# The first W1 piece loaded ahead of the second x half, and five units' first slab done in column halves

## The chip, the cores and the metric

The kernel runs on one core of one Trainium2 chip. The metric is the device time of one execution in microseconds, the median of several runs. Engines: PE (matmul), DVE and ACT (elementwise, both can read PSUM), POOL (elementwise), SP (issues the DMAs). PE writes to PSUM, which has 8 banks of 512 fp32 columns; the next matmul into a bank has to wait until its content has been copied out.

## What is computed

The input x has 2048 rows (tokens) of D = 512. Two branches are mixed by a gate for each token:

```python
g = sigmoid((x * gate_w).sum(-1, keepdims=True))
# a: linear attention, 32 heads of 16
q, k, v = split(x @ wqkv)                       # per head
phi = lambda t: concat(softmax(t @ w_phi), softmax(-(t @ w_phi)))
kv, z = phi(k).T @ v, phi(k).sum(tokens)        # per head
a = concat_heads((phi(q) @ kv) / (phi(q) @ z + 1e-6)) @ wo
# b: dense branch, Dff = 1376
b = relu(x @ w1) @ w2
out = g * a + (1 - g) * b
```

All inputs and the output are bf16.

## The kernel before

The program is planned engine by engine. `p.op(engine, fn, after, ev)` appends one instruction to an engine's list, with the events it waits for and the event it sets; `p.dma` does the same for a DMA issue. Each engine runs its list strictly in the order of the calls, so an instruction that waits holds up everything behind it on its engine. `p.early(engine)` moves what was listed so far on that engine ahead of the engine's wait in the start barrier. `free[bank]` names the event after which a PSUM bank may be written again.

The tokens are handled in four chunks of 512 columns of XT, which is x transposed (four blocks `t` or `dt` of 128 rows of D). Chunks 1 to 3 are transposed by DMA. Chunk 0, which the kernel starts with, is transposed on PE: x is loaded row-wise into XS in two halves `h` (256 tokens each, `loadx0`, L162), PE multiplies blocks of 128 x 128 with an identity matrix into PSUM (`xtr`, L239), and DVE (L255) or ACT (L258) copy them into XT as bf16. There are 16 such transposes, 8 for each half of x. Until the first half of x is there, PE runs matmuls on a constant tile (`warm`, L232).

Then comes the dense branch of chunk 0 for its first eight units `u` of 128 columns of W1: `slab(t)` (L528) runs, for one block `t` of D, one 512-column matmul for each unit, into the bank `UB[u]`, where

```python
UB = (3, 4, 5, 0, 6, 7, 2, 1)
```

Four slabs accumulate in the eight banks; in slab 0 a unit first has to wait until its bank's transposes have been copied out. W1 comes in pieces (`loadw1`, L166): the columns of units 0 to 3 of block 0 (event `w10a`), those of units 4 to 7 of block 0 (`w10`), then blocks 1 to 3 one by one. After slab 3 `relu` copies each bank to HT, and the rest follows: further units (`hunit`, L282), v (`vtile`, L411), the products of weights (`pre`, L316), attention tiles (`atile`, L336), and at the end the output products (`finB`, L490, and `finA`, L499).

The order on PE in the opening is: five warm matmuls, the gate column (L225), one more warm matmul, six transposes of the first half of x, two of the second, two of the first, four of the second, slab 0 for units 0 to 3, the last two transposes of the second half, slab 0 for units 4 to 7, slabs 1 to 3. The transposes lie in banks 6, 7, 2, 1 and again 2, and DVE and ACT make three copies each: DVE of 256 columns each, ACT of 256, 512 and 512.

Of the kernel before, what the change touches and what calls it, by code (L numbers as in the profile page):

```python
# [5 lines left out]
ACT = mybir.ActivationFunctionType  # L6
# [62 lines left out]
def bass_gated_mix__linear_kernel_hedgehog__dense_activation_relu__prompt_kernel(  # L69
# [17 lines left out]
    P = 128  # L87
    NT = S // P
    NDT = D // P
# [15 lines left out]
    with ExitStack() as es:  # L105
        E = es.enter_context
        XT = E(nc.sbuf_tensor("XT", [P, NDT, S], BF16))
# [6 lines left out]
        W1 = E(nc.sbuf_tensor("W1", [P, NDT, DFF + 8], BF16))  # L114
# [11 lines left out]
        IDN = E(nc.sbuf_tensor("IDN", [P, P], BF16))  # L126
# [14 lines left out]
        PS = E(nc.psum_tensor("PS", [P, 8, 512], FP32))  # L141

        XS = OT[:, 0, :].rearrange("p (j d) -> p j d", j=4)
# [7 lines left out]
        p = _Plan(["sp", "pool", "act", "dve", "pe"])  # L151
        free = {b: [] for b in range(8)}
# [8 lines left out]
        def loadx0(h):  # L161
            p.dma("sp", lambda e: e.dma_start(out=XS[:, 2 * h:2 * h + 2, :], in_=xq[:, 2 * h:2 * h + 2, :]),  # L162
                  f"x0{h}", ev=f"x0{h}")

        def loadw1(t, c0=0, c1=DFF, tag=""):
            p.dma("sp", lambda e: e.dma_start(  # L166
                out=W1[:, t, c0:c1], in_=B_w1[t * P:(t + 1) * P, c0:c1]), f"w1{t}{tag}", ev=f"w1{t}{tag}")
# [1 line left out]
        p.dma("act", lambda e: e.dma_start(out=GR[0:NDT, :], in_=gate_w.rearrange("(j p) -> j p", p=P)),  # L169
              "gr", after=["grz"], ev="gr")  # L170
        p.early("act")
        for h in range(2):
            loadx0(h)
        p.early("sp")
        loadw1(0, 0, 4 * P, "a")
        loadw1(0, 4 * P, 8 * P)
        for t in range(1, NDT):
            loadw1(t, 0, 8 * P)
        p.dma("sp", lambda e: e.dma_start(
            out=W1[:, :, 8 * P:DFF], in_=B_w1[:, 8 * P:DFF].rearrange("(j p) n -> p j n", p=P)), "w1r", ev="w1r")  # L180
        p.dma("sp", lambda e: e.dma_start(
            out=WPS[:, :, :], in_=A_w_phi.rearrange("(g hl) r c -> (hl r) g c", g=NDT)), "wps", ev="wps")
        p.dma("sp", lambda e: e.dma_start(
            out=WV[:, :, :], in_=A_wqkv[:, 2 * D:3 * D].rearrange("(j p) n -> p j n", p=P)), "wv", ev="wv")
        for i in range(2):
            p.dma("sp", lambda e, i=i: e.dma_start_transpose(
                out=WQKT[:, 4 * i:4 * i + 4, :], in_=A_wqkv[:, i * D:(i + 1) * D]), f"wqk{i}", ev=f"wqk{i}")
        for c in range(1, NCH):
            p.dma("sp", lambda e, c=c: e.dma_start_transpose(
                out=XT[:, :, c * 512:(c + 1) * 512], in_=x2[c * 512:(c + 1) * 512, :]), f"x{c}", ev=f"x{c}")  # L190
# [9 lines left out]
            after=["wps"], ev="wd")  # L200
        for gt in range(NDT):
# [4 lines left out]
                after=["wd", "m8"], ev=f"wbd{gt}")  # L206
# [5 lines left out]
             after=["iota0"], ev="idn")  # L212
        p.op("dve", lambda e: e.tensor_single_scalar(ROW8[:, :], ROW8[:, :], 4, ALU.arith_shift_right),
             after=["iota"], ev="r8")
# [3 lines left out]
             after=["r64"], ev="m32")  # L218

        def xready(c):  # L220
            return ["xa0", "xa1", "xa2", "xb0", "xb1", "xb3"] if c == 0 else [f"x{c}"]

        def gatecol(bank):
            gp = PS[:, bank, 0:NDT]
# [5 lines left out]
        def warm(n, cols=512):  # L230
            for _ in range(n):
                p.op("pe", lambda e: e.matmul(PS[:, 4, 0:cols], ones[:, 0:P], ones[:, 0:cols], start=True, stop=True),  # L232
                     after=["one"])

        def xtr(nm, h, dts, bank, evacs, part=None):
            n = 2 * len(dts)
            for i in (range(n) if part is None else part):
                dt, j = dts[i // 2], 2 * h + i % 2
                p.op("pe", lambda e, i=i, dt=dt, j=j: e.matmul(  # L239
                    PS[:, bank, i * P:(i + 1) * P], XS[:, j, dt * P:(dt + 1) * P], IDN[:, :],  # L240
                    start=True, stop=True),
                    after=["idn", f"x0{h}"] + (free[bank] if i == 0 else []), ev=(f"xt{nm}" if i == n - 1 else None))
            if part is not None and n - 1 not in part:
                return []
            return xev(nm, h, dts, bank, n, evacs)

        def xev(nm, h, dts, bank, n, evacs):
            src = PS[:, bank, 0:n * P].rearrange("p (t c) -> p t c", c=256)
            out = []
            for eng, i0, i1, ev in evacs:  # L250
                d = XT[:, dts[i0]:dts[i0] + i1 - i0, h * 256:(h + 1) * 256]
                s = src[:, i0:i1, :]
                if eng == "dve":
                    out.append(lambda d=d, s=s, ev=ev: p.op(
                        "dve", lambda e: e.tensor_copy(d, s), after=[f"xt{nm}"], ev=ev))  # L255
                else:
                    out.append(lambda d=d, s=s, ev=ev: p.op(
                        "act", lambda e: e.activation(d, s, ACT.Copy), after=[f"xt{nm}"], ev=ev))  # L258
            free[bank] = [evacs[-1][3]]
            return out  # L260

        w1all = ["w10a", "w1r"] + [f"w1{t}" for t in range(NDT)]

# [15 lines left out]
        def hunit(c, kt, eng="act", bank=None):  # L279
            bank = nextbank() if bank is None else bank  # L280
            for t in range(NDT):
                p.op("pe", lambda e, t=t: e.matmul(  # L282
                    PS[:, bank, :], W1[:, t, kt * P:(kt + 1) * P], XT[:, t, c * 512:(c + 1) * 512],
                    start=(t == 0), stop=(t == NDT - 1)),
                    after=(xready(c) + w1all + free[bank] if t == 0 else ()),
                    ev=(f"h{c}_{kt}" if t == NDT - 1 else None))
            relu(c, kt, bank, eng)

        def rest(c):
            bank = nextbank()  # L290
            for i in range(4):
                for s in range(NDT):
                    t0 = c * 512 + i * P
                    p.op("pe", lambda e, i=i, s=s, t0=t0: e.matmul(  # L294
                        PS[:, bank, i * P:i * P + NR + 1], XT[:, s, t0:t0 + P], W1[:, s, KU * P:DFF + 1],
                        start=(i == 0 and s == 0), stop=(s == NDT - 1), skip_group_check=True),
                        after=(xready(c) + w1all + ["gw"] + free[bank] if i == 0 and s == 0 else ()),
                        ev=(f"h{c}_r" if i == 3 and s == NDT - 1 else None))
            src = PS[:, bank, :].rearrange("p (i n) -> p i n", i=4)
            b = c % 2  # L300
            p.op("act", lambda e: e.activation(HR[:, b, :, 0:NR], src[:, :, 0:NR], ACT.Relu),
                 after=[f"h{c}_r"] + ([f"hr{c - 2}"] if c >= 2 else []), ev=f"rr{c}")
            p.op("act", lambda e: e.activation(
                EG[:, 4 * c:4 * c + 4].unsqueeze(2), src[:, :, NR:NR + 1], ACT.Exp, scale=-1.0), ev=f"eg{c}")
            free[bank] = [f"eg{c}"]
            p.dma("sp", lambda e: e.dma_start_transpose(
                out=HT[:, KU, c * 512:(c + 1) * 512].rearrange("p (i t) -> p i t", i=4),
                in_=HR[:, b, :, :].rearrange("p i n -> p (i n)")), f"hr{c}", after=[f"rr{c}", f"hz{b}"], ev=f"hr{c}")
# [20 lines left out]
        def atile(m):  # L329
            b = m % NB  # L330
            first = xready(m // 4) + ([f"pc{i}" for i in range(8)] if m == 0 else [])
            order = [(dt, w) for dt in range(NDT) for w in range(2)]
            if m - 1 in split:
# [186 lines left out]


        UB = (3, 4, 5, 0, 6, 7, 2, 1)
        XA = ("xa0", "xa1", "xa2", "xa2")
        XB = ("xb0", "xb1", "xb1", "xb3")

        def slab(t, us=range(8)):
            for u in us:
                p.op("pe", lambda e, u=u: e.matmul(  # L528
                    PS[:, UB[u], :], W1[:, t, u * P:(u + 1) * P], XT[:, t, 0:512],
                    start=(t == 0), stop=(t == NDT - 1)),  # L530
                    after=["w10a" if t == 0 and u < 4 else f"w1{t}", XA[t], XB[t]] + free[UB[u]],
                    ev=(f"h0_{u}" if t == NDT - 1 else None))

        warm(5)
        p.early("pe")
        gatecol(3)
        warm(1, 384)
        ea = xtr("a0", 0, (0, 1), 6, (("dve", 0, 1, "xa0"), ("dve", 1, 2, "xa1")))
        c1 = ("a1", 0, (2, 3), 7, (("act", 0, 2, "xa2"),))
        xtr(*c1, part=(0, 1))  # L540
        eb = xtr("b0", 1, (0,), 2, (("act", 0, 1, "xb0"),))
        ec = xtr(*c1, part=(2, 3))
        ed = xtr("b1", 1, (1, 2), 1, (("act", 0, 2, "xb1"),))
        for fn in (ea[0], eb[0], ea[1], ec[0], ed[0]):
            fn()
        slab(0, range(4))
        for fn in xtr("b2", 1, (3,), 2, (("dve", 0, 1, "xb3"),)):
            fn()
        slab(0, range(4, 8))
        for b in range(VB):  # L550
            p.op("dve", lambda e, b=b: e.memset(VS[:, b, :, 64:65], 1.0), ev=f"one{b}")
        for b in range(2):
# [30 lines left out]
        for m in range(NT):  # L583
# [7 lines left out]
            if m == 3:  # L591
                for a, b in ((0, 4), (4, 7), (7, KU)):
                    p.dma("sp", lambda e, a=a, b=b: e.dma_start(
                        out=W2[:, a:b, :], in_=B_w2[a * P:b * P, :].rearrange("(j p) n -> p j n", p=P)),
                        "w2", ev=f"w2{a}")
                p.dma("sp", lambda e: e.dma_start(out=W2[0:NR, KU, :], in_=B_w2[KU * P:DFF, :]), "w2", ev="w2")
            if m == 5:
                for a in range(0, NDT, 2):
                    p.dma("sp", lambda e, a=a: e.dma_start(
                        out=WO[:, a:a + 2, :], in_=A_wo[a * P:(a + 2) * P, :].rearrange("(j p) n -> p j n", p=P)),  # L600
# [70 lines left out]
```

The softmax here doesn't subtract the row's maximum and nothing guards it: scores larger than these inputs give would overflow.

## Time and profile before

| | us |
|---|---|
| median of five runs | 147.23 |
| the runs | 147.17, 147.21, 147.23, 147.58, 147.77 |
| the profiled execution, its own time | 147.23 |
| its span, first to last instruction | 145.9 |
| PE busy in the span | 142.5 (98%) |
| DVE busy | 93.0 (64%) |
| ACT busy | 72.2 (49%) |
| POOL busy | 52.1 (36%) |

Times in the profile are counted from the first instruction of the span. A line such as L528 is a line of the kernel before. In the chain of work each row is a start, a length, and the engine and line that the end of the kernel hung on at that time; "issue" is time in which the engine waited for nothing that the profile shows. In the timeline a row is a start, the length from the first start to the last end of the instructions merged in it, engine, line, operation, what it writes and reads, shapes and count, and in brackets how long the engine was idle before and what released it. PE's instructions overlap in such rows, since a matmul's record includes its way through the array. SPq is SP's issuing of DMAs; "to landing" is from the issue's start until the data is there. A row in the list of waits is the engine and line that waited, what released it, and total, number and longest wait.

### The profile page before, as it was taken

How to read it: one execution, taken by the hardware profiler on the slowest of the kernel's cores; microseconds unless marked ns; L12 is line 12 of the kernel's file. 1: busy time of each engine (PE TensorE's matmuls, PEld its weight loads, DVE VectorE, ACT ScalarE, POOL GpSimd, SP SyncE). 2: the span in 40 equal slices, each digit the busy share in tenths (PEclk: the TensorE clock that was granted, in tenths of full speed). 3: DMA queues.
4: the chain of work that ended last, by engine and by line, in shares of the span. 5: the costliest groups of instructions: out<-in, count | busy, mean ns of one | idle time of the engine just before them, and what ended most of it. 6: DMA issues, size and time to landing. Idle time of an engine off the chain costs nothing.

```text
span 145.9 us, 2520 instructions
## 1 busy us (share of the span) xinstructions
PE 142.5 (98%) x961; PEld 73.2 (50%) x978; DVE 93.0 (64%) x158; ACT 72.2 (49%) x124; POOL 52.1 (36%) x62
## 2 busy tenths in 40 slices
PE   8999999999999999999999999999999999999994
PEld 4544744444456455544645555554444444444442
DVE  3428838777687878678698967664445555555342
ACT  3306737788778778797878862022211111111150
POOL 2040003778868678688869810200000000000000
DMA  6999992123349973325733431354242222322213
GB/s 193 311 262 205 179 229 58 27 45 76 72 97 362 125 211 77 72 63 108 79 72 87 92 72 39 73 108 126 59 106 73 72 72 66 82 72 74 72 46 104
DMA packets 45221, 16.12 MB, mean 110 GB/s; under 512 B 39352, under 2 KB 44568, under 8 KB 45208
## 3 DMA queue, kind: packets, MB, share of 16 engines
q1 hardware_dynamic: 45056, 15.92, 48.8%
q8 instruction: 8, 0.13, 0.4%
q10 hardware_dynamic: 152, 0.03, 0.1%
q14 instruction: 5, 0.04, 0.1%
HBM read 4.41 MB, written 2.10 MB: 45 GB/s over the span
## 4 chain that ended last, share of the span: by engine, by line
PE 97%; DVE 1%; issue 1%; DVEq 0%
PE PS L490 25%; PE PS L282 19%; PE PS L336 18%; PE PS L499 9%; PE PS L411 9%; PE PS L528 5%; PE PS L465 3%; PE PS L433 3%; PE PS L294 2%; PE PS L232 2%; PE PS L316 1%; PE PS L239 1%; DVE WQK L513 1%; DVE XT L255 0%; PE PS L225 0%
## 5 line engine op out<-in xcount | busy, mean ns | idle before, releaser
L490 PE MATMUL PS<-W,HT 128*128 128x512 bf16 (+4 forms) x181 | 40.0, 366 | 0.3
L355 ACT ACTIVATE EB<-PS 128x480 bf16<-128x480 f32 (+1 forms) x44 | 30.1, 757 | 15.9 <-PE PS L336 15.9
L379 POOL TENSOR_TENSOR EB<-EB,SC 128x1024 bf16<-128x1024 bf16 x15 | 28.9, 1928 | 24.4 <-DVE SC L377 24.4
L504 ACT ACTIVATE TFA<-PS,GT 128x512 bf16<-128x512 f32 x16 | 11.0, 687 | 42.7 <-PE PS L499 42.7
L282 PE MATMUL PS<-XT,W 128*128 128x512 bf16 x124 | 30.0, 379 | 0.2
L336 PE MATMUL PS<-WQK,XT 128*128 128x480 bf16 x128 | 28.5, 366 | 0.0
L513 DVE SCALAR_TENSOR_TENSOR WQK<-PS,OMG,TFA 128x512 bf16<-128x512 f32 (+2 forms) x17 | 12.2, 719 | 23.6 <-ACT TFA L504 22.4
L375 DVE TENSOR_REDUCE ZB<-EB 128x64 f32<-128x1024 bf16 x15 | 18.3, 1220 | 13.8 <-ACT EB L355 13.8
L490 PEld LDWEIGHTS PS<-W,HT 128*128 128x128 bf16 (+1 forms) x187 | 17.0, 98 | 17.4
L268 ACT ACTIVATE HT<-PS 128x512 bf16<-128x512 f32 x35 | 20.3, 616 | 7.0 <-PE PS L528 5.1
L336 PEld LDWEIGHTS PS<-WQK,XT 128*128 128x128 bf16 x128 | 12.5, 98 | 13.8
L390 DVE TENSOR_REDUCE ZB<-EB 128x64 f32<-128x1024 bf16 x16 | 18.7, 1168 | 0.0
L282 PEld LDWEIGHTS PS<-XT,W 128*128 128x128 bf16 x128 | 12.0, 98 | 13.2
L399 POOL TENSOR_TENSOR EB<-EB,SC 128x512 bf16<-128x512 bf16 x16 | 16.9, 1056 | 1.3
L499 PE MATMUL PS<-WO,OT 128*128 128x512 bf16 x63 | 16.0, 378 | 0.1
L411 PE MATMUL PS<-WV,XT 128*128 128x512 bf16 x59 | 15.3, 379 | 0.3
L475 DVE TENSOR_TENSOR WQK<-PS,RDEN 128x512 bf16<-128x512 f32 x16 | 11.1, 691 | 0.5
L499 PEld LDWEIGHTS PS<-WO,OT 128*128 128x128 bf16 x64 | 6.1, 97 | 7.2
L377 DVE RECIPROCAL SC<-ZB 128x64 f32<-128x64 f32 x16 | 8.8, 553 | 0.5
L411 PEld LDWEIGHTS PS<-WV,XT 128*128 128x128 bf16 x64 | 5.5, 97 | 4.9
L421 ACT ACTIVATE VS<-PS 128x512 bf16<-128x512 f32 x13 | 8.0, 612 | 0.0
L465 PEld LDWEIGHTS PS<-KVNZ,PHQ 128*128 128x128 bf16 x128 | 6.1, 97 | 3.6
(57 smaller groups left out, 88.8 us busy)
## 6 DMA issues: line engine op xcount, KB each, us to landing
out_dram<-WQK SPq DMA_DIRECT2D x15, 128.0 KB, 1.7
W<-in_B_w_dram SPq DMA_DIRECT2D x3, 256.0 KB, 4.5
W<-in_B_w_dram SPq DMA_DIRECT2D x2, 384.0 KB, 5.1
OT<-in_A_x_dram SPq DMA_DIRECT2D x2, 256.0 KB, 2.8
WV<-in_A_wqkv_dram SPq DMA_DIRECT2D x1, 512.0 KB, 6.1
W<-in_B_w_dram SPq DMA_DIRECT2D x1, 512.0 KB, 4.3
WO<-in_A_wo_dram SPq DMA_DIRECT2D x2, 256.0 KB, 3.6
W<-in_B_w_dram SPq DMA_DIRECT2D x1, 352.0 KB, 5.5
```

Source lines behind the costliest of these rows:

```text
L268: p.op("act", lambda e: e.activation(dst, src, ACT.Relu), after=[f"h{c}_{kt}"], ev=ev)
L282: p.op("pe", lambda e, t=t: e.matmul(PS[:, bank, :], W1[:, t, kt * P:(kt + 1) * P], XT[:, t, c * 512:(c + 1) * 512], start=(t == 0), stop= ...
L336: p.op("pe", lambda e, dt=dt, which=which: e.matmul(PS[:, which, 0:DE], XT[:, dt, m * P:(m + 1) * P], WQK[:, which, dt * DE:(dt + 1) * DE] ...
L355: p.op("act", lambda e: e.activation(dst, s_, ACT.Exp, scale=scale), after=[f"qk{m}"] + busy, ev=ev)
L375: p.op("dve", lambda e: e.tensor_reduce(zk, ek, AX.X, ALU.add), after=[emk, f"cst{b}"], ev=f"zk{m}")
L379: p.op("pool" if m < NT - 1 else "dve", lambda e: e.tensor_tensor(EB[:, b, 3, :].rearrange("p (g f) -> p g f", f=DH), EB[:, b, 2, :].rearr ...
L390: p.op("dve", lambda e: e.tensor_reduce(ZB[:, b, 0:64].rearrange("p (h s) -> p h s", s=2), bass.AP(tensor=EB, offset=base, ap=[[EBS, P], [ ...
L399: p.op("pool", lambda e: e.tensor_tensor(EB[:, b, 0, :].rearrange("p (h s f) -> p h s f", h=H, s=2)[:, :, 1, :], EB[:, b, 1, :].rearrange( ...
L411: p.op("pe", lambda e, dt=dt: e.matmul(PS[:, bank, :], XT[:, dt, m * P:(m + 1) * P], WV[:, dt, :], start=(dt == 0), stop=(dt == NDT - 1)), ...
L490: p.op("pe", lambda e, kt=kt, M=M: e.matmul(PS[:, bank, 0:n], HT[0:M, kt, m * P:(m + 1) * P], W2[0:M, kt, cs], start=(kt == 0), stop=(kt = ...
L499: p.op("pe", lambda e, t=t: e.matmul(PS[:, bank, :], OT[:, t, m * P:(m + 1) * P], WO[:, t, :], start=(t == 0), stop=(t == NDT - 1)), after ...
L513: p.op("dve", lambda e: e.scalar_tensor_tensor(out=OSB[:, ob, cs], in0=PS[:, bank, 0:n], scalar=OMG[:, m:m + 1], in1=TFA[:, m % 2, cs], op ...
```

## The change

Loads: the order of issue on SP was first x half, second x half, (start barrier,) first W1 piece, second W1 piece. It becomes first x half, first W1 piece, (start barrier,) second x half, second W1 piece. The rest is as it was.

Transposes: all eight of the first x half come first, into banks 6 (block 0), 7 (block 1) and 5 (blocks 2 and 3); then units 0 to 3 do slab 0 for the first 256 columns; then all eight transposes of the second half go into banks 2, 1 and 7 (blocks 2 and 3); then unit 4 does its first 256 columns of slab 0, units 0 to 4 do their second 256, and units 5 to 7 their whole 512. Slabs 1 to 3 are unchanged. DVE and ACT copy the blocks in this order: of the first half DVE blocks 0 and 1, ACT blocks 2 and 3 in one; of the second half ACT block 0, DVE block 1, ACT blocks 2 and 3 in one. Each copy waits for its own blocks' transposes alone.

```diff
-        for h in range(2):
-            loadx0(h)
+        loadx0(0)
+        loadw1(0, 0, 4 * P, "a")
         p.early("sp")
-        loadw1(0, 0, 4 * P, "a")
+        loadx0(1)
         loadw1(0, 4 * P, 8 * P)
...
+        def xtr(h, dt, bank, off):
+            for i in range(2):
+                j = 2 * h + i
+                p.op("pe", lambda e, i=i, j=j: e.matmul(
+                    PS[:, bank, off + i * P:off + (i + 1) * P], XS[:, j, dt * P:(dt + 1) * P], IDN[:, :],
                     start=True, stop=True),
+                    after=["idn", f"x0{h}"] + (free[bank] if i == 0 else []), ev=(f"xt{h}{dt}" if i else None))
+
+        def xev(eng, h, dt, n, bank, off):
+            d = XT[:, dt:dt + n, h * 256:(h + 1) * 256]
+            s = PS[:, bank, off:off + n * 256].rearrange("p (t c) -> p t c", c=256)
+            ev = f"xv{h}{dt}"
+            if eng == "dve":
+                p.op("dve", lambda e: e.tensor_copy(d, s), after=[f"xt{h}{dt + n - 1}"], ev=ev)
+            else:
+                p.op("act", lambda e: e.activation(d, s, ACT.Copy), after=[f"xt{h}{dt + n - 1}"], ev=ev)
+            free[bank] = [ev]
...
+        VD = (0, 1, 2, 2)
+
+        def slab(t, us=range(8), half=None):
+            c0, c1 = (0, 512) if half is None else (half * 256, half * 256 + 256)
             for u in us:
                 p.op("pe", lambda e, u=u: e.matmul(
+                    PS[:, UB[u], c0:c1], W1[:, t, u * P:(u + 1) * P], XT[:, t, c0:c1],
+                    start=(t == 0 and half != 1), stop=(t == NDT - 1), skip_group_check=True),
+                    after=["w10a" if t == 0 and u < 4 else f"w1{t}"] + (free[UB[u]] if half != 1 else [])
+                    + [f"xv{h}{VD[t]}" for h in range(2) if half in (None, h)],
                     ev=(f"h0_{u}" if t == NDT - 1 else None))
...
-        ea = xtr("a0", 0, (0, 1), 6, (("dve", 0, 1, "xa0"), ("dve", 1, 2, "xa1")))
-        c1 = ("a1", 0, (2, 3), 7, (("act", 0, 2, "xa2"),))
-        xtr(*c1, part=(0, 1))
-        eb = xtr("b0", 1, (0,), 2, (("act", 0, 1, "xb0"),))
-        ec = xtr(*c1, part=(2, 3))
-        ed = xtr("b1", 1, (1, 2), 1, (("act", 0, 2, "xb1"),))
-        for fn in (ea[0], eb[0], ea[1], ec[0], ed[0]):
-            fn()
-        slab(0, range(4))
-        for fn in xtr("b2", 1, (3,), 2, (("dve", 0, 1, "xb3"),)):
-            fn()
-        slab(0, range(4, 8))
+        TA = ((6, 0), (7, 0), (5, 0), (5, 256))
+        TB = ((2, 0), (1, 0), (7, 0), (7, 256))
+        for dt in range(NDT):
+            xtr(0, dt, *TA[dt])
+        xev("dve", 0, 0, 1, 6, 0)
+        xev("dve", 0, 1, 1, 7, 0)
+        xev("act", 0, 2, 2, 5, 0)
+        slab(0, range(4), 0)
+        for dt in range(NDT):
+            xtr(1, dt, *TB[dt])
+        xev("act", 1, 0, 1, 2, 0)
+        xev("dve", 1, 1, 1, 1, 0)
+        xev("act", 1, 2, 2, 7, 0)
+        slab(0, (4,), 0)
+        slab(0, range(5), 1)
+        slab(0, (5, 6, 7))
```

More of the change, by code (lines that the diff above doesn't have):

```diff
@@ L220, in xready @@
         def xready(c):
-            return ["xa0", "xa1", "xa2", "xb0", "xb1", "xb3"] if c == 0 else [f"x{c}"]
+            return ["xv00", "xv01", "xv02", "xv10", "xv11", "xv12"] if c == 0 else [f"x{c}"]
         def gatecol(bank):
@@ L233, in warm @@
                      after=["one"])
[L235 to L240, printed above, removed]
-                    start=True, stop=True),
[L242 to L260, printed above, removed]
+        def xtr(h, dt, bank, off):
[3 more added lines that the diff above has]
+                    PS[:, bank, off + i * P:off + (i + 1) * P], XS[:, j, dt * P:(dt + 1) * P], IDN[:, :],
+                    start=True, stop=True),
+                    after=["idn", f"x0{h}"] + (free[bank] if i == 0 else []), ev=(f"xt{h}{dt}" if i else None))
@@ L522, in bass_gated_mix__linear_kernel_hedgehog__dense_activation_relu__prompt_kernel @@
         UB = (3, 4, 5, 0, 6, 7, 2, 1)
-        XA = ("xa0", "xa1", "xa2", "xa2")
-        XB = ("xb0", "xb1", "xb1", "xb3")
-        def slab(t, us=range(8)):
+        VD = (0, 1, 2, 2)
+        def slab(t, us=range(8), half=None):
+            c0, c1 = (0, 512) if half is None else (half * 256, half * 256 + 256)
             for u in us:
                 p.op("pe", lambda e, u=u: e.matmul(
-                    PS[:, UB[u], :], W1[:, t, u * P:(u + 1) * P], XT[:, t, 0:512],
-                    start=(t == 0), stop=(t == NDT - 1)),
-                    after=["w10a" if t == 0 and u < 4 else f"w1{t}", XA[t], XB[t]] + free[UB[u]],
+                    PS[:, UB[u], c0:c1], W1[:, t, u * P:(u + 1) * P], XT[:, t, c0:c1],
+                    start=(t == 0 and half != 1), stop=(t == NDT - 1), skip_group_check=True),
+                    after=["w10a" if t == 0 and u < 4 else f"w1{t}"] + (free[UB[u]] if half != 1 else [])
+                    + [f"xv{h}{VD[t]}" for h in range(2) if half in (None, h)],
                     ev=(f"h0_{u}" if t == NDT - 1 else None))
```

## The prediction

> **What bounds the kernel now.** I read the page first, then the chain of waits, then what the tensor engine (PE) waited for, then the timeline between 2.8 and 7 us in narrow windows, and last the loads' landing times. From the page, and from the list of who waited for whom, cut to PE:
>
> ```profile
> PE 97%; DVE 1%; issue 1%; DVEq 0%
> PE PS L232 <- DVE ONE L208: 0.4, 1, 0.4
> ```
>
> The chain that ended last is PE from end to end, and from the list PE has no named wait after its first one at 0.4 us. So whatever the opening gains or loses comes out at the end one for one: no later wait of PE is there to swallow it. The opening, from the chain in order of time:
>
> ```profile
> 3.21 1.32 PE PS L239 x14
> 4.53 0.10 issue
> 4.62 1.02 PE PS L528 x4
> 5.65 0.13 PE PS L239 x2
> 5.77 0.02 issue
> 5.80 0.42 DVE XT L255
> 6.22 0.05 DVE VS L551 x2
> 6.28 0.00 issue
> 6.28 4.49 PE PS L528 x20
> ```
>
> L239 are the transposes of x, L528 the matmuls of the W1 slabs, L255 and L258 the copies of transposed x from PSUM to XT on DVE and ACT. From 6.28 on PE runs through. Before that there are two holes, and the timeline gives their edges:
>
> ```profile
> 3.67 0.42 DVE L255 CAST XT<-PS 128x256 bf16<-128x256 f32 x1 [0.59 <-PE PS L239]
> 4.10 0.38 ACT L258 ACTIVATE XT<-PS 128x256 bf16<-128x256 f32 x1 [1.69 <-PE PS L239]
> 4.31 0.22 PE L239 MATMUL PS<-IDN,OT 128*128 128x128 bf16 x1
> 4.62 0.38 PE L528 MATMUL PS<-XT,W 128*128 128x512 bf16 x1
> 4.85 0.60 ACT L258 ACTIVATE XT<-PS 128x512 bf16<-128x512 f32 x1
> 5.49 0.27 PE L239 MATMUL PS<-IDN,OT 128*128 128x128 bf16 x2
> 5.60 0.60 PE L528 MATMUL PS<-XT,W 128*128 128x512 bf16 x2
> 5.80 0.42 DVE L255 CAST XT<-PS 128x256 bf16<-128x256 f32 x1 [1.37 <-PE PS L239]
> ```
>
> **Units read from these rows.** A matmul's record ends later than its successor starts, so I use distances between starts. Four 512-column matmuls and the next start: (5.49 - 4.62)/4 = 0.217; in the long run of slabs 0.215. A transpose (128 columns): (5.60 - 5.49)/2 = 0.055 there, but early DVE was released by the fourth transpose (3.67) and ACT by the eighth (4.10): (4.10 - 3.67)/4 = 0.107. The pitch halves near 4.2 us, although the windows' granted clock reads 1.00 throughout. A 256-column matmul has no row; its ends are 0.055 (128 columns) and 0.215 (512). The rows between are straight in columns (L336, 480 columns: 1.62/8 = 0.203), so I take 0.108. From a transpose's end to its copy's start: 5.49 + 0.27 = 5.76 to 5.80, 0.04. From a copy's end to the waiting matmul: 5.80 + 0.42 = 6.22 to 6.28, 0.06; 0.14 at 4.62, where several semaphores are waited for. A copy of 512 columns on ACT 0.60 (0.59 for its other row), of 256 on ACT 0.38, on DVE 0.42.
>
> So the holes of before are 4.62 - (4.31 + 0.06) = 0.25 and 6.28 - (5.60 + 2 x 0.215) = 0.25. Slab 0 ends, and slab 1 starts, at 6.28 + 2 x 0.215 = 6.71. All the change can win by filling holes is 0.50.
>
> **Loads.** Four SP issues change order, not number:
>
> ```profile
> 0.08 0.87 SPq L162 DMA_DIRECT2D OT<-in_A_x_dram  x2
> 1.09 2.23 SPq L166 DMA_DIRECT2D W<-in_B_w_dram  x5
> L166 SPq DMA_DIRECT2D W<-in_B_w_dram x1: 431/431/431, 1.5 to 1.5; - x1
> DMA to landing us min/median/max: 4.1/4.1/4.1
> ```
>
> The first half of x lands at 2.8 as before. The first W1 piece, issued now at 0.5 instead of 1.1, takes the second x half's place, so it lands by 3.4 (that half's old landing, with twice the bytes) and not before 2.8; PE wants it at 3.9. The second x half goes behind it and behind SP's start gate, is issued at about 1.0 and lands between 3.4 (its old landing) and 4.1 (the W1 piece's old landing, which had the same bytes in front); I take the later end, and PE wants it at 5.0. Both are covered by the transposes, with 0.5 and 0.9 us to spare; beyond that lateness costs one for one. The second W1 piece and everything after it has the same issues and bytes ahead, and lands as before at 1.5 + 4.1, read finely 5.55.
>
> **PE's order.** Columns are unchanged; five of the eight matmuls of slab 0 become ten half ones: five more matmuls and weight loads. Ten times 0.108 is five times 0.215, and loads (0.10 each in their own row) lie under the previous matmul, as they do under 128-column transposes spaced 0.055. Price 0, up to 5 x (0.215 - 0.108) = 0.5 if halves cost more than columns say.
>
> The Trainium skill speaks against this in "TensorE: Matmul & The Clock Gate", section "Back-to-back issue gap": in a stream of weight loads and matmuls it gives about 81 ns a matmul at 128 columns and 131 at 512. Interpolated, two halves would cost some 65 ns more than one whole, 0.3 us for five units. The trace has 55 and 215 instead, straight in columns, so the trace is followed.
>
> **Walk through the new order.** The first eight transposes are all of the first x half, at the same pace, so their ends are those of before: the second releases DVE at 3.67 - 2 x 0.107 = 3.46, and the copy ends at 3.88; the eighth releases ACT at 4.10. ACT's copy there is now the 512-column one out of bank 5: 4.10 + 0.59 = 4.69. Units 0 and 1 (banks 3 and 4) do first halves from about 3.95 to 4.30, the first at the slow pitch. Unit 2 sits in bank 5, and its matmul waits until that ACT copy has emptied the bank: 4.69 + 0.06 = 4.75. This is the wait that the change adds, 0.45 of idle PE, and in PE's order behind it stand unit 3, all eight transposes of the second half, and through these every second-half copy.
>
> From there: two halves to 4.75 + 0.22 = 4.97; eight transposes to 4.97 + 0.44 = 5.41. The second of them ends at 4.97 + 0.06 + 0.22 = 5.25; ACT copies that block from 5.29 to 5.67; second halves can start at 5.73. Unit 4's first half stands in between and needs the second W1 piece (5.55): 5.60 to 5.71, so it lies inside the wait for ACT. If that piece came after 5.62, this cover would be gone and all behind it would slip equally. Five second halves: 5.73 + 0.54 = 6.27. Unit 5 needs bank 7, emptied by ACT's last copy: the eighth transpose ends 4.97 + 7 x 0.055 + 0.22 = 5.58, copy from 5.62 to 6.22, so 6.28: no more than 0.01 late. Units 5 to 7: 6.28 + 3 x 0.215 = 6.92. Against 6.71 that is +0.2. Both holes of before are gone, and about 0.1 (before 3.95), 0.45 (bank 5) and 0.3 (second half's first copy, partly filled by unit 4) come in their place. Seven half matmuls lie on this path: with the ends 0.055 and 0.215 for one, the sum would be -0.2 or +0.9.
>
> ACT and DVE copy the same columns as before; their orders change, and the fills behind DVE's last copy start earlier. In slabs 1 to 3 PE still waits for nothing: the third W1 block of 5.55 to 7.6 keeps its landing, and PE comes later. The relu copies and SP's later transposes shift with PE. Zero, by the list of waits above.
>
> The profiled execution took 147.23, its span 145.9 with 1.3 around it, and the median of five runs is also 147.23: 147.23 + 0.2 = 147.43.
>
> **Rivals.**
>
> *Slower, the second W1 piece.* Place: unit 4's first half, which now stands ahead of five second halves instead of behind the first four units. Before, a later landing had 0.25 of cover in the hole at 6.03; now it has 0.07. It decides from a landing after 5.62. The nearest later row is the next W1 block, at 6.3: price 6.3 - 5.62 = 0.7, so 148.1. For: three of the runs lie at 147.2, but two at 147.6 and 147.8, so something moves; against: nothing ahead of this piece grows. Chance 0.18.
>
> *Slower, the clock.* The pitch fell to 0.055 only 3.8 us after PE's first matmul at 0.4. If 0.45 of idle right behind it set PE back to the slow pitch, and the rise took those 3.8 again, half of it would be lost: 1.9, so 149.3. Against: the pitch is still 0.215 after the 0.25 hole. Chance 0.07. The same page, section "Part 1: The HAM clock gate", has a window of about 3.4 us which must be idle before the clock falls; no run here shows so long a hole.
>
> *Faster, the wait for bank 5 isn't last.* Were ACT's copy early enough and unit 2 unhindered, halves would fill the holes: at most -0.5, 146.7. The order written for bank 5 speaks against it; and even with unit 2 free, unit 4 still waits for 5.55, and the tail is the same. Chance 0.1.
>
> *The planned forecast*, 147.43, own range 147.1 to 147.7: 0.65.
>
> **How the numbers follow.** About 0.3%, 0.44 us, is what a measurement of this kernel can tell from no change. The forecast, +0.2, is within it, save 0.05 where halves or latencies cost 0.25 more. The W1 rival passes the bound in 0.13 of its 0.18, the clock always, the faster rival in 0.08 of 0.1. Faster 0.08; slower 0.05 + 0.13 + 0.07 = 0.25; within it 0.67. The range 147.0 to 148.1 holds forecast and W1 rival and leaves out the other two, 0.17.
>
> **What would show it.** In the changed profile: ACT's first copy a 512-column one at 4.10; PE idle from about 4.30 to 4.75 ahead of the third half matmul; second halves from 5.73, released by ACT; slab 1 starting at 6.92. Slab 1 before 6.5 would say that the wait for bank 5 was not binding; half matmuls spaced by much more than 0.108, that the loads aren't hidden; a pitch of 0.43 for 512 columns after 4.75, the clock.

## The result

The changed kernel took 148.03 us (median of 43 runs, 147.30 to 148.88) against 147.44 of before (80 runs, 146.99 to 148.21): ratio 1.0038, interval 1.0028 to 1.0048. The forecast was 147.43, 0.2 above the 147.23 that before had then; measured is 0.6 above the median of before from the same comparison. The profiled execution is the third fastest of the 43, 147.40 with a span of 146.1, 0.17 above the profiled one of before. So the trace explains 0.17, and the question is what the other executions lose.

The chain in order of time, after (L238 are now the transposes, L250 ACT's copies, L519 the slabs):

```profile
3.11 0.91 PE PS L238 x8
4.02 0.02 issue
4.04 0.61 ACT XT L250
4.65 0.05 issue
4.69 0.39 PE PS L519 x2
5.09 0.45 PE PS L238 x8
5.53 0.11 PE PS L519
5.64 0.03 issue
5.67 4.18 PE PS L519 x21
```

And what PE's weight loads waited for at the slabs (total, times, longest):

```profile
PEld PS L519 <- ACT XT L250: 0.9, 2, 0.6
```

This is the predicted walk: ACT's 512-column copy out of bank 5 from 4.04, PE held by it until 4.69 (foreseen 4.75), eight transposes, unit 4's first half, second halves from 5.67 (5.73). Slab 1's first matmul starts at 6.88 (6.92), against 6.72 before.

### The profile page after: what moved, and what is told of

The parts are those of the page before. It is cut to its first block, busy times and chain, and to the rows that moved or that the text cites. A ratio compares the mean times of both kernels' runs of the same rounds, so it can differ in the third digit from the quotient of the medians.

```text
span 146.1 us, 2529 instructions
## 1 busy us (share of the span) xinstructions
PE 142.6 (98%) x966; PEld 73.2 (50%) x983; DVE 93.0 (64%) x158; ACT 72.4 (50%) x124; POOL 52.0 (36%) x62
## 4 chain that ended last, share of the span: by engine, by line
PE 97%; issue 1%; DVE 1%; ACT 0%; DVEq 0%
PE PS L481 25%; PE PS L273 19%; PE PS L327 18%; PE PS L490 9%; PE PS L402 9%; PE PS L519 5%; PE PS L456 3%; PE PS L424 3%; PE PS L285 2%; PE PS L232 2%; PE PS L307 1%; PE PS L238 1%; DVE WQK L504 1%; ACT XT L250 0%; PE PS L225 0%
## 5 line engine op out<-in xcount | busy, mean ns | idle before, releaser
L327 PE MATMUL PS<-WQK,XT 128*128 128x480 bf16 x128 | 28.5, 366 | 0.0
L327 PEld LDWEIGHTS PS<-WQK,XT 128*128 128x128 bf16 x128 | 12.5, 98 | 13.8
L519 PE MATMUL PS<-XT,W 128*128 128x512 bf16 (+1 forms) x36 | 7.7, 356 | 0.3 <-ACT XT L250 0.2
```

The costliest lines, as they stand in the source:

```text
L327: p.op("pe", lambda e, dt=dt, which=which: e.matmul(PS[:, which, 0:DE], XT[:, dt, m * P:(m + 1) * P], WQK[:, which, dt * DE:(dt + 1) * DE] ...
L519: p.op("pe", lambda e, u=u: e.matmul(PS[:, UB[u], c0:c1], W1[:, t, u * P:(u + 1) * P], XT[:, t, c0:c1], start=(t == 0 and half != 1), stop ...
```

## A measure for the single traces

Every run below left one trace, so the loss can be located execution by execution. From slab 1 on PE runs through: own time less the start of slab 1's first matmul is 147.23 - 6.72 = 140.51 before, 147.40 - 6.88 = 140.52 after, and between 140.50 and 140.53 in five more traces with the same work behind slab 1 (e0, e1, e3, e7, e8). What an execution loses it loses ahead of slab 1, except where a wait further down is named (e2, e4 and the kernels that move the v tiles).

Five theories: X, the second x half comes late; W, the second W1 piece comes late for unit 4; T, the second transposed load of wqkv binds further down; K, the clock's rise at a random time; H, the new hole delays that rise.

## The experiments

**e0, the changed kernel again**, for a second trace.

> The changed kernel once more, unedited, for a second trace and as the mate of the next three. Its first trace ran by the predicted walk (slab 1 at 6.88 against 6.72 before, its own time 147.40 against 147.23), but the median of its runs is 148.03 against 147.44: 0.17 of the 0.6 is explained, 0.4 is not. Theory X (second x half late: it landed at 4.53 in the first trace, 0.39 before PE wanted it at 4.92, where it had landed at 3.44 before): a slower execution shows PE idle ahead of the ninth transpose. Theory W (second W1 piece late: 5.14, wanted at 5.37): PE idle ahead of unit 4's first half beyond 5.6. Theory T (the second transposed load of wqkv late: 16.18, wanted at 16.22, where before it had 15.22 and 16.07): PE idle around 16.2 and nothing different before. All expect a ratio of 1.003 to 1.005.

Measured: 147.92 against 147.31, ratio 1.0028 (1.0010 to 1.0046). Its chain, from the window 4 to 8:

```profile
1.47 4.17 DMA W<-in_B_w_dram
5.63 0.05 issue
5.68 2.34 PE PS L519 x13
```

A row "DMA" runs from issue to landing. Here the chain goes through the second W1 piece: it lands at 5.63 instead of 5.14, and PE, free from 5.33, waits for it with unit 4's first half while the second halves stand behind. Slab 1 starts at 7.00, 0.12 later than in the first trace. Theory W, small in this execution.

**e1, unit 4 whole.**

```diff
-        slab(0, (4,), 0)
-        slab(0, range(5), 1)
-        slab(0, (5, 6, 7))
+        slab(0, range(4), 1)
+        slab(0, (4, 5, 6, 7))
```

> Unit 4 is not halved: units 0 to 3 do their second halves right after the second half's transposes, units 4 to 7 follow whole, so that the second W1 piece is wanted at about 6.1 instead of 5.37. By the rows of the first trace: second halves from 5.67, four of them to 6.11, four whole matmuls to 6.97, so slab 1 0.1 later than in the changed kernel. Theory W: the median nevertheless falls by 0.2 to 0.4 below the changed kernel's. Theories X and T: the median rises by 0.1.

Measured: 147.72, ratio 1.0027 (1.0007 to 1.0047). The median is 0.2 below e0's, as W expects, but the intervals lie on each other; the timing decides nothing. In its trace the clock was late (half matmuls 0.17 to 0.22 apart until 5.3, transposes 0.107 until 5.7) and slab 1 starts at 7.48, although the piece landed at 5.19, long before unit 4 wanted it: this lateness is not theory W.

**e2, the changed order on PE with the loads of before.**

```diff
-        loadx0(0)
-        loadw1(0, 0, 4 * P, "a")
+        for h in range(2):
+            loadx0(h)
         p.early("sp")
-        loadx0(1)
+        loadw1(0, 0, 4 * P, "a")
```

> The changed order on PE with the order of loads of before: both x halves ahead of the start barrier, the first W1 piece behind it. The first W1 piece then lands near 4.06 instead of 3.24; unit 0 starts at 4.1 instead of 3.97, and since units 0 and 1 are through by 4.45, the wait for bank 5 until 4.69 hides that; the walk is the same, slab 1 at 6.9. Theory X: the second x half lands at 3.4 again and the median falls by 0.3 to 0.4, to a ratio of about 1.001. Theories W and T: the median stays within 0.1 of the changed kernel's.

Measured: 147.72, ratio 1.0018 (1.0000 to 1.0037), the lowest of the single edits, but not apart from 1.0038 beyond the intervals. In its trace the second x half landed at 4.00, the second W1 piece at 4.69, earlier than in any trace with the new load order; slab 1 starts at 6.79, 0.07 after the first trace of before, which is less than the openings of before differ among themselves. Units 0 to 3 waited here for the first W1 piece (4.34), not for bank 5. The median is 0.2 to 0.3 below the changed kernel's two, but since both the x half and the second W1 piece came early, the time doesn't tell theory X from W. Later this execution lost 0.3 in front of the second transposed load of wqkv (16.4).

**e4, other banks**, so that units 0 to 3 find empty ones.

```diff
-        UB = (3, 4, 5, 0, 6, 7, 2, 1)
+        UB = (3, 4, 5, 0, 2, 6, 7, 1)
...
-        TA = ((6, 0), (7, 0), (5, 0), (5, 256))
-        TB = ((2, 0), (1, 0), (7, 0), (7, 256))
+        TA = ((6, 0), (7, 0), (2, 0), (2, 256))
+        TB = ((6, 0), (7, 0), (1, 0), (1, 256))
```

> The changed kernel with other banks: transposes of the first half in banks 6, 7 and 2, of the second in 6, 7 and 1, and the units in banks 3, 4, 5, 0, 2, 6, 7, 1, so that units 0 to 3 find four empty banks and none waits for ACT's 512-column copy. By the first trace's rows: first halves 3.97 to 4.47, the second x half (4.53) then binds, transposes 4.58 to 5.03, ACT's copy 4.90 to 5.28, second halves from 5.34 to 5.88, units 5 to 7 to 6.53, and slab 1 at the landing of its W1 block, 6.6: 0.25 before the changed kernel's, 0.1 before the old one's. That is the profile by the walk, if the wait for bank 5 was what cost. If it wasn't the wait, slab 1 stays at 6.88. Theory X: the median gains less than the profile, 0 to 0.1, since the second x half now binds in every execution; theories W and T: the median falls by 0.2 to 0.25.

Measured: 147.87, ratio 1.0024 (1.0006 to 1.0041). Four first halves now follow each other without a wait for ACT, yet slab 1 starts at 6.85, not 6.6: the clock rose only at 5.1, so they took 0.17 to 0.21 each, and the second halves could start only at 5.65, behind ACT's copy (to 5.59; the second W1 piece, at 5.45, was there before). So the hole for bank 5 could be taken away and little came of it in this execution. The chain between 12 and 20:

```profile
10.51 6.23 DMA PHQ<-in_A_wqkv_dram
16.74 0.04 issue
16.78 1.01 PE PS L307 x16
```

The second transposed load lands at 16.74, and the weight loads of the products (L307) stand 0.6 in front of it; by own time less slab 1 (147.86 - 6.85 = 141.01) the execution lost 0.5 there. Hence theory T, which the next two test.

**e5 and e6, a v tile ahead of the second four weight products**, in the changed kernel and in before.

```diff
+        vtile(1, "dve")
         for i in range(4, 8):
             pre(i)
-        vtile(1, "dve")
```

> The changed kernel with the second v tile (four matmuls, 0.86) moved ahead of the second four weight products on PE, so that these want the second transposed load of wqkv 0.86 later, at about 17.1 instead of 16.2. In the traces so far that load landed at 15.2 (before), 16.2, 15.7, 15.7, 16.4 and 16.7, and in the last two PE stood 0.3 and 0.6 in front of it. Theory T (this load binds in most executions, of both kernels, and eats what the opening wins): the median falls by 0.2 to 0.4 against the changed kernel's (ratio to before 0.999 to 1.002), and no wait for that load is left in the trace. Theory K (the clock's rise, which came at 4.2, by 4.7, by 3.9, 5.7, by 4.4 and 5.1 in the traces, decides): no change beyond 0.1.

> The same move of the second v tile in the kernel before. Theory T: the runs above 147.4 (half of them) come down, the median falls by 0.1 to 0.2, ratio 0.9985 to 0.9995, less than in the changed kernel, since before wants the load at 16.07 and its trace had it at 15.2. Theory K: no change, ratio 1.0.

Measured: 148.39, ratio 1.0049 (1.0032 to 1.0067; six runs), and 147.80, 1.0015 (0.9996 to 1.0034): neither falls. The move had a price that I had not counted: one v tile does not cover the copies of the products, and the weight loads of the first attention tile (L327) wait for DVE, here e5's list:

```profile
PEld PS L519 <- DMA W<-in_B_w_dram: 0.9, 1, 0.9
PEld PS L327 <- DVE WQK L312: 0.7, 1, 0.7
```

The 0.7 is the wait of the weight loads, which run ahead of PE; own time less slab 1 is 148.41 - 7.65 = 140.76 in e5 and 147.94 - 7.19 = 140.75 in e6, so the price is 0.24. The mean of e6 lies 0.25 above the mean of the runs of before beside it, which leaves nothing for theory T; that of e5 0.75, 0.2 more than the 0.56 of the changed kernel, which leaves 0.05.

The edit lies behind slab 3, so the opening of e5's trace is one more of the changed kernel, and it shows theory W at its full size. The chain from 3 on:

```profile
1.47 4.82 DMA W<-in_B_w_dram
6.29 0.05 issue
6.33 4.28 PE PS L519 x22
```

PE stands 0.9 in front of unit 4's first half, and slab 1 starts at 7.65, 0.8 later than in the first trace.

**e7, the hole filled** with three matmuls on constants.

```diff
-        slab(0, range(4), 0)
+        slab(0, (0, 1), 0)
+        for _ in range(3):
+            p.op("pe", lambda e: e.matmul(PS[:, 1, 0:P], ones[:, 0:P], ones[:, 0:P], start=True, stop=True))
+        slab(0, (2, 3), 0)
```

> The changed kernel with three 128-column matmuls on constants, into the still empty bank 1, between units 1 and 2 of the first halves, where PE otherwise stands 0.4 to 0.5 us for bank 5. They take 0.17 at the fast pitch and 0.32 at the slow one, so they fit. Theory H (the hole that the change makes falls into the time in which the clock has yet to rise, and delays the rise): the fast pitch comes by 4.3 and the median falls by 0.2 to 0.4. Theory K (the rise comes at random, whatever the hole): no change beyond 0.1. Theory T: no change.

Measured: 147.90, ratio 1.0022 (1.0006 to 1.0038). PE's timeline:

```profile
4.52 0.52 PE L539 MATMUL PS<-ONE 128*128 128x128 bf16 x3
4.86 0.61 PE L519 MATMUL PS<-XT,W 128*128 128x256 bf16 x2
5.27 1.03 PE L238 MATMUL PS<-IDN,OT 128*128 128x128 bf16 x8
6.12 0.51 PE L519 MATMUL PS<-XT,W 128*128 128x256 bf16 x3
```

The hole is filled, and eight transposes still take (6.12 - 5.27)/8 = 0.106 each; the fast pitch comes at about 6.1. So the late rise needs no hole. In the three traces without the hole for bank 5 (e4, e7 and e11) the fast pitch came at 5.1, 6.1 and 5.9, in the four unedited ones with it by 3.9 (e0), 4.7 (the first), 4.8 (e5) and at about 6 (e10): nothing speaks for theory H, though so few traces, and a median 0.1 below the changed kernel's, don't exclude a small part. Slab 1 starts at 7.65 here, as late as in e5, although the second W1 piece (6.06) was there before PE came to unit 4 (6.12): a late clock alone costs an execution as much as a late piece.

**e3, the load order alone**, on PE's old order (the diff of e2 reversed, applied to before).

> The new order of loads alone, on PE's old order. The second x half lands at about 4.5 instead of 3.4, and the old order wants it for its seventh transpose at 3.5: PE stands 0.9 to 1.0 there. By the rows: seventh transpose at 4.55, ACT's copy of it to 5.25, slab 0 from 5.3, unit 6 from 7.0 after DVE's last copy, slab 1 at 7.4 instead of 6.7: ratio 1.004 to 1.006. It says that the load order without the new PE order is a loss; theory T expects somewhat less, 1.002 to 1.004, because executions in which the later load binds anyway hide a part.

Measured: 149.14, ratio 1.0082 (1.0050 to 1.0114). The direction is as expected, the size was missed: the second x half came at 5.03, PE stood 1.4 for it, and the clock stayed slow beyond 8, so slab 1 starts at 9.07. Whether so long a hole puts the rise off, no other run tests. Twelve runs fall in two groups, five at 147.9 to 148.1 and seven at 149.1 to 149.8. The loads and PE's order belong together.

**e8, a first piece for five units**, so that unit 4 no longer needs the second.

```diff
-        loadw1(0, 0, 4 * P, "a")
+        loadw1(0, 0, 5 * P, "a")
...
-        loadw1(0, 4 * P, 8 * P)
+        loadw1(0, 5 * P, 8 * P)
...
-                    after=["w10a" if t == 0 and u < 4 else f"w1{t}"] + ...
+                    after=["w10a" if t == 0 and u < 5 else f"w1{t}"] + ...
```

> The changed kernel with the first W1 piece one unit wider (columns of units 0 to 4, the second piece those of 5 to 7). PE's order and its work are the same; only unit 4's first half no longer waits for the second piece, which in the traces with the new load order landed at 5.1 to 6.3 (with the old order 4.7 to 5.6), and which is now wanted first at about 6.2. Theory W: the median falls by 0.2 to 0.3 below the changed kernel's (147.9 to 148.0), to a ratio of 1.001 to 1.002, and the trace has no wait for W1 ahead of the second halves. Theories T and K: no change beyond 0.1. The wider piece delays the second x half by about 0.1, which is a little against it: up to 0.05.

Measured: 147.86, ratio 1.0029 (1.0006 to 1.0051). The trace has no wait for W1 left (slab 1 at 7.04, with a late clock), but the expected fall of 0.2 to 0.3 isn't seen: 1.0029 is below 1.0038 by less than half of its interval's half width, and not below e0's 1.0028. In this trace the second piece was there at 4.99, before PE came to unit 4 (5.45). With a spread of 0.4 among executions, twelve runs can't tell.

**e9 and e10, the v tiles moved with a cover**, in before and in the changed kernel.

```diff
+        vtile(1, "dve")
         for i in range(4, 8):
             pre(i)
-        vtile(1, "dve")
         vtile(2, "dve", nextbank())
+        vtile(3)
...
-            if m + 3 < NT:
+            if 0 < m < NT - 3:
                 vtile(m + 3)
```

> The kernel before with the second v tile ahead of the second four weight products, and the fourth v tile drawn ahead of the first attention tile, so that two v tiles again cover the copies of those products (in the earlier trial 0.7 was lost there). The second transposed load of wqkv is wanted 0.86 later. Theory T: the median falls by 0.1 to 0.25 below that of before (ratio 0.998 to 0.999). Otherwise: 1.000.

> The same move in the changed kernel. Theory T (that load decides also where the changed kernel loses more than its first trace shows): the median falls by 0.2 to 0.4, ratio 1.000 to 1.002. Theory W or K alone: no change beyond 0.1, ratio 1.003 to 1.004.

Measured: 147.57, ratio 1.0016 (0.9998 to 1.0035), and 148.18, 1.0042 (1.0020 to 1.0064). Again the weight loads stand 0.7, now because the second attention tile waits for ACT's exponentials, here e9's list:

```profile
PEld PS L336 <- ACT EB L355: 0.7, 1, 0.7
```

Own time less slab 1's start is 147.47 - 6.63 = 140.84 in e9 and 148.45 - 7.56 = 140.89 in e10, 0.33 and 0.37 above the unedited kernels': the price of the move in these traces, not 0.7. The mean of e9 is only 0.11 above that of before (147.57 against 147.46), that of e10 0.64 above it, 0.08 more than the changed kernel's 0.56. So by this pair the load of wqkv may take about 0.2 from an average execution of before and 0.3 from one of the changed kernel; by e5 and e6 it takes next to nothing from either. Both pairs leave it at most about 0.1 of the difference between the kernels; that is argued, with prices from single traces. The opening of e10, again the changed kernel's:

```profile
1.47 4.73 DMA W<-in_B_w_dram
6.20 0.05 issue
6.24 1.91 PE PS L519 x11
```

And ACT's last copy in it, which empties bank 7 for unit 5:

```profile
6.19 0.60 ACT L250 ACTIVATE XT<-PS 128x512 bf16<-128x512 f32 x1 [0.26 <-PE PS L238]
```

**e11, all three edits** (e4, e8 and e10 together).

> The changed kernel without all three suspected waits: other banks, so that units 0 to 3 find empty ones; the first W1 piece for five units; the v tiles drawn ahead of the weight products. By the rows: slab 1 at 6.5 to 6.6, the landing of its W1 block, 0.1 to 0.2 before the old kernel's 6.7. If the three waits are the whole of the loss, the ratio is 0.998 to 1.000; if the clock's late rise or another load is behind a part of it, 1.001 to 1.003.

Measured: 147.48, ratio 1.0005 (0.9980 to 1.0030), with 0.24 of it paid for the v tiles (147.85 - 7.10 = 140.75 in its trace). Less that price, 0.0016, it would be 0.999, as expected if the three waits are the whole of the loss; the interval covers the other case too. Its interval and the changed kernel's (1.0028 to 1.0048) hardly overlap, which is so for no single edit of that kernel. So the loss is no longer seen with all three removed, but the run doesn't say which of them made it. Before isn't beaten; no version tried was shown to be faster.

## Why the prediction was right, and where it was short

**The range and the sum.** The measured median, 148.03, lies in the range on record, 147.0 to 148.1, but outside the planned forecast's own 147.1 to 147.7, and the difference of 0.59 passes the 0.44 within which the prediction put 0.67 of its chance. The direction was right and the sum too small by 0.4; the base, 147.23 for 147.44, makes the other 0.2. The range held because it took in the price of the W1 rival, 148.1, to which the prediction gave only 0.18.

**The walk through PE's new order** held in the profiled execution. The marks on PE's path came within 0.06 of their forecast: 4.69 for 4.75, 5.67 for 5.73, 6.88 for 6.92. The wait for bank 5 was there (by PE's starts idle from 4.14 + 0.11 to 4.69, 0.44 for 0.45; somewhat less if the second of these half matmuls still ran at the slow pitch), with everything behind it. Half matmuls were spaced 0.109 (estimated 0.108), so the trace was rightly preferred to the 81 and 131 ns of the Trainium skill ("TensorE: Matmul & The Clock Gate", "Back-to-back issue gap"). The sum, +0.2, is what the two profiled executions differ by (0.17). That they agree so well is partly luck: in this execution the clock rose by 4.7 and the second W1 piece came at 5.14, so that unit 4's first half ran at 5.37 for 5.60, inside the wait for ACT, and cost nothing.

**The term that was mis-sized** is in the part on loads: "the second W1 piece and everything after it has the same issues and bytes ahead, and lands as before at 1.5 + 4.1". The issue did stay at 1.47. But the landing moved: with the old load order 5.55, 4.99, 5.01 and 4.69 (before, e6, e9, e2), mean 5.1; with the new one 5.14, 5.63, 5.19, 5.45, 6.29, 6.06, 6.14 and 6.20 (after, e0, e1, e4, e5, e7, e3, e10), mean 5.8. The second x half went the same way: foreseen at 4.1 at the latest, it came at 4.24 to 5.03 in the same eight traces. Equal bytes ahead were not an equal landing. (With the wider first piece, and so a narrower second one, it came at 4.99 in e8 and 5.72 in e11.) The DMA rate between 3.5 and 5.0, the last number of the row, is 243 GB/s in before and 136 in e10:

```profile
3.50:5.00 1.50, 1.40 (x14) 1.08 (x12) 0.76 (x2) 0.90 (x3) 0.00 (x0) 1.00 0.91 243
```

```profile
3.50:5.00 1.50, 1.36 (x9) 0.62 (x8) 0.66 (x2) 0.60 (x1) 0.00 (x0) 1.00 0.86 136
```

It is 255, 279 and 256 in e6, e9 and e2, and 136 to 226 in all eight traces with the new order and the same pieces, so the dip goes with that order; with the wider first piece it is 181 in e11 but 259 in e8. Why less is moved then, no run settles.

**What the rival on the W1 piece said** happened in some executions. Its turning point was a landing after 5.62; of the four openings of the changed kernel, three lie beyond it (5.63, 6.20, 6.29), and all three chains go through this load. Slab 1 starts at 6.88, 7.00, 7.56 and 7.65 in these four (the first, e0, e10, e5), mean 7.27, and at 6.72, 7.19 and 6.63 in three openings of before, mean 6.85: 0.42 more, and the means of all runs differ by 0.56 (148.10 against 147.54).

What the late piece adds is less than its wait, because ACT's copies hold PE too. Without it second halves could start 0.05 after ACT's first copy of the second half, and unit 5 after its last one: by these rows the piece costs 0.16 in e0 and 0.71 in e5, but only 0.06 in e10, where the transposes ran at the slow pitch until 5.9, ACT emptied bank 7 at 6.79 and unit 5 started at 6.91 (there the late clock alone would have brought nearly the same). That is 0.23 on average, most of it from one trace; with the walk's 0.17 it makes up 0.40 of the 0.42, the late clock standing in both groups of openings (e6 and e10).

So that the late piece holds single executions up is shown; that it makes up most of the rest of the median's loss is argued from four traces. The timed runs agree for all three waits together (e11), but e1 and e8, which take away this one, are not below e0 beyond the noise. Some 0.1 to 0.2 stays open.

**The second x half** being late cost nothing directly: no unedited opening of the changed kernel waits for it at the ninth transpose; in e11, with the banks of e4, it did bind: it landed at 4.87, and the ninth transpose started at 4.92, some 0.15 after PE was free.

**The clock**, the prediction's second rival, was not thrown back to the slow pitch in any trace once it was fast. Its late rise, which the prediction has nowhere in its sum, moves single executions of both kernels, with the hole or without it: the fast pitch came at 3.2 in e9, 4.2 in before, 5.5 in e6, about 6 in e10 and e11. The forecast's base, five runs and one trace with an early rise, lay towards the fast end; over 80 runs before has 147.44.

## What to carry to other kernels

Ask of a reordered in-order queue not only what binds now, but how much slack each load has at its new place, and how far its landing scatters: a matmul moved ahead of five others gave up the 0.25 of cover that the hole behind it had been, and a landing that varies by 1.1 us then cost between nothing and 0.7 of an execution. Equal bytes ahead of a load do not promise an equal landing. Where the openings of single executions scatter by more than the effect, compare marks in several traces (here the start of slab 1, which gives the own time to 0.02 where nothing waits behind it) before trusting a median of twelve. And a chain that goes through a load does not say what the load costs: look for the wait that would have come next.

## What the runs showed of the hardware

The same second W1 piece, issued at 1.47 each time, landed between 5.14 and 6.29 with one and the same load order, and the second transposed load of wqkv between 14.95 and 16.74. The time of the clock's rise, read from the spacing of transposes (0.107, then 0.055), varied between 3.2 and about 6.1 after a first matmul at 0.38 to 0.39 in every trace; in e3, with 1.4 of idle PE from 3.7, it came at 8.3. Five traces keep a record of the granted clock, and it begins at 3.21 (e9), 3.90 (e0), 4.29 (e2), 4.83 (e5) and 8.34 (e3), where the spacing turns; ahead of it, and in the other traces, there is no record, and the column in the windows reads 1.00 all the same. The Trainium skill ("TensorE: Matmul & The Clock Gate", "Part 1: The HAM clock gate") tells of a free-running window as the reason, which would fit, though its half microsecond of scatter is less than these traces show.
